# Routed experts in row blocks of 128, with one half of an expert's sums under the other

## The chip, the cores and the metric

One core of one Trainium2 chip runs the whole program; the other cores are idle. The metric is device time of one execution in microseconds (us). An execution of the kernel before took 560.33 us (median of 3 runs, 559.5 to 560.93).

## The reference

Three stages follow each other, on 1536 tokens (2 batches of 768) of 512 numbers:

```
attention   8 heads of 64; key j counts for query i if j < 4 or 0 <= i - j < 128; softmax; times v
dense       h = x @ w_in [512 x 2048];  g = max(0.01 h, h);  x = g @ w_out [2048 x 512]     (weights in float64)
routed      do = x @ w_skip > 0;  e = argmax(x @ w_gate) of 8 experts;  p = softmax(x @ w_gate)[e]
            out = x + p * (max(x @ w1[e], 0) @ w2[e])   for tokens with do, else out = x
            w1[e] 512 x 1024, w2[e] 1024 x 512
```

## The kernel before, in words

The program is first planned, then written out. Each piece of work is an operation with an engine, a modelled cost, a priority (`pr`, the lowest goes first), what it reads and writes, and buffers by tag; `Plan.run` walks a model of the five queues and emits operations in the order in which the model starts them. Each engine runs its own list in that order on the chip, whatever the real times are. So an operation that is late holds up everything behind it on its engine.

**Precision.** A product of two fp32 tensors is made from three fast products: each operand is split into a high part (a rounding copy, mostly on ACT) and a low part (the difference, on DVE or POOL): high x high, high x low, low x high. `split` (L693) does this for weights in SBUF, its copy at L701 and its difference at L708; `split_psum` (L1091) does it for tensors in PSUM, both at L1094 and L1095.

**Dense part.** Tokens go through in six groups of 256. For each group `chunk` (L822) runs 16 steps over the hidden columns: sums of `h` (L835), the activation, then sums into `acc` (L856). Attention of the next group is laid between the steps. After each group `gating` (L886) decides where its two tiles of 128 tokens go. It transposes x (L918), splits it (L921, L922), makes nine scores per token with `w9` (L930; one column for `w_skip`, eight for `w_gate`, 12 products a tile: three per 128 rows), copies them (L935), transposes them back (L937), and works out on DVE, in small steps (L947 to L992), the expert, the gate and the rank of each token among those of its expert, from counts that PE makes (L977). Tokens are then scattered by an indirect DMA of POOL into `scr`, 128 rows for each expert.

**The last group** (g = 5) is gated one tile at a time, on the way to the first expert. Expert 0's rows aren't read back from `scr`: `first_rows` (L801) loads those of the earlier groups, `first_x` (L810) adds the new ones on PE. Each of four column blocks `x0` gets a product of the rows loaded (L817), and one for each of the two new tiles, with a 0/1 matrix `sel` of that tile (L819). `sel` comes from DVE (L987) out of the ranks (L983). A plain fp32 product of PE stands in the trace as two instructions.

**Routed part** (`plan_routed`, L1019), eight experts one after the other: sums g1 of expert e, `hp` (L1066, two halves `a` of 512 columns, four blocks `k` of 128 rows, 24 products), the relu into `hs` (first half ACT L1070, second half DVE L1071), eight transposes (L1075, in two groups of four), the split into `gt`, the sums g2 into `yp` (L1082, 24 products), and the end: gate times `yp` plus x (L1085) and an indirect DMA to the output (L1087). Transposes of x for the next expert are L1059. Priorities put g1 of expert e + 1 ahead of g2 of expert e, and the transposes of `hs` between the second and third quarter of that g2.

**Weights of the experts** come in four tiles of 512 KB for each matrix (L1037), into raw buffers (`wm` four, `vs` one, `wf` one in two halves), and are split into pairs of `w` buffers. There are 32 `w` buffers, room for four matrices; the dense weights hold them until the last group's steps let them go. The order is W1 of expert 0, W1 of 1, W2 of 0, W1 of 2, W2 of 1, and so on; the low part of the last tile of a matrix is POOL's, the others are DVE's. A tile of w1 holds rows k, 4 + k, 8 + k, ... (partition p has row 4p + k), and of w2 partition p has rows 8p + 2n and 8p + 2n + 1. So all that meets them is cut with the same stride:

```
src = io["moe2_w2"][e].rearrange("(p j) d -> p j d", j=8) if m else io["moe2_w1"][e].rearrange("(p k) f -> p k f", k=4)
... tp.tile[:, k, :], xs.tile[:, k:512:4], c["idt"]          (x of an expert, L1059)
... tp.tile[:, j, :], hs.tile[:, 4 * b + j:1024:8], c["idt"]  (hs, L1075: both groups of four need both halves)
```

Of the kernel before, what the change touches and what calls it, by code (L numbers as in the profile page):

```python
# [225 lines left out]
class Arm:  # L226
# [63 lines left out]
    def keep(self):  # L290
# [7 lines left out]
        self.w9 = k("w9", [128, 2, 4, 9], F32R)  # L298
# [394 lines left out]
    def split(self, src, dst, at, n, pr, hi="ACT", lo="DVE", view=lambda t: t):  # L693
# [13 lines left out]
        P.op(hi, {"ACT": c_act(n, False), "DVE": c_dve2(n), "POOL": c_pool1(n)}[hi], f_hi, r=[src], w=[hk], pr=pr)  # L707
# [156 lines left out]
    def prepare(self, done):  # L864
# [9 lines left out]
        P.op("DVE", 90, lambda: nc.vector.tensor_copy(self.w9[:, 0], raw.tile), r=[raw], w=["w9"], pr=8)  # L874
        P.op("DVE", 100, lambda: nc.vector.tensor_tensor(out=self.w9[:, 1], in0=raw.tile, in1=self.w9[:, 0].bitcast(F32), op=ALU.subtract), r=[raw], w=["w9"], pr=8)
# [10 lines left out]
    def gating(self, g, acc, own):  # L886
# [9 lines left out]
        for i, t in zip(own, tiles):  # L896
            x = P.buf("x2", [128, 514])
            x2.append(x)
            for h in range(parts):
                q = slice(w * h, w * h + w)  # L900
                if (i if n > 1 else h) == 0:
                    P.op("ACT", c_act(w, True), lambda x=x, i=i, q=q: nc.scalar.activation(out=x.tile[:, q], in_=acc[i].tile[:, q], func=AF.Copy), r=[acc[i]], w=[(x, h)], pr=pr - 8)
                else:
                    P.op("DVE", c_dve(w), lambda x=x, i=i, q=q: V.tensor_copy(x.tile[:, q], acc[i].tile[:, q]), r=[acc[i]], w=[(x, h)], pr=pr - 8)
# [3 lines left out]
        lp = P.buf("T", [9, 128 * n])  # L908
        for m, x in enumerate(x2):
# [14 lines left out]
            for h in range(parts):  # L924
                ks = range(4 // parts * h, 4 // parts * (h + 1))

                def lg(m=m, xh=xh, ks=ks):
                    for k in ks:
                        for j, (a, b) in enumerate(((0, 0), (1, 0), (0, 1))):
                            nc.tensor.matmul(out=lp.tile[:, 128 * m:128 * m + 128], lhsT=self.w9[:, a, k, :], rhs=xh.tile[:, b, 128 * k:128 * k + 128],  # L930
                                             start=k == 0 and j == 0, stop=k == 3 and j == 2)

                P.op("PE", 3 * len(ks) * 54, lg, r=[(xh, (0, h)), (xh, (1, h)), "w9"], w=[lp], pr=pr)
        ls = P.buf("wl", [9, 128 * n])
# [13 lines left out]
        d(70, lambda: V.tensor_scalar(out=v(act, 1), in0=lt.tile[:, :, 0:1], scalar1=0.0, scalar2=None, op0=ALU.is_gt), [lt], [(s, "act")])  # L948
        for m in range(n):
            d(80, lambda m=m: V.scalar_tensor_tensor(out=cand()[:, m, :], in0=lt.tile[:, m, 1:9], scalar=one(mx, m), in1=c["em"][:, 0, :], op0=ALU.is_equal, op1=ALU.mult),  # L950
              [lt, (s, "mx")], [(s, ("cand", m))])
# [467 lines left out]
```

## Time and profile before

| | us |
|---|---|
| median of 3 runs (lowest, highest) | 560.33 (559.5, 560.93) |
| the profiled execution | 561.0 |
| its span, first to last instruction | 559.2 |
| PE busy in it | 521.8 (93%) |
| DVE, ACT, POOL busy | 415.9, 345.8, 166.9 |

The profile is one execution; its span is 1.8 us less than its time. Busy times of PE are those of matmuls (weight loads stand beside them as PEld). A line of a timeline merges like instructions that follow each other: its start, the time from there to the end of the last, and in brackets how long the engine had been idle and which instruction of another engine let it go on. The granted clock of PE is a share of full speed, 1.00 for 2.4 GHz and 0.50 for 1.2 GHz.

### The profile page before, as it was taken

How to read it: one execution, taken by the hardware profiler on the slowest of the kernel's cores; microseconds unless marked ns; L12 is line 12 of the kernel's file. 1: busy time of each engine (PE TensorE's matmuls, PEld its weight loads, DVE VectorE, ACT ScalarE, POOL GpSimd, SP SyncE). 2: the span in 40 equal slices, each digit the busy share in tenths (PEclk: the TensorE clock that was granted, in tenths of full speed). 3: DMA queues.
4: the chain of work that ended last, by engine and by line, in shares of the span. 5: the costliest groups of instructions: out<-in, count | busy, mean ns of one | idle time of the engine just before them, and what ended most of it. 6: DMA issues, size and time to landing. Idle time of an engine off the chain costs nothing.

```text
span 559.2 us, 10360 instructions
## 1 busy us (share of the span) xinstructions
PE 521.8 (93%) x3370; PEld 457.7 (82%) x3370; DVE 415.9 (74%) x1167; ACT 345.8 (62%) x899; POOL 166.9 (30%) x288
## 2 busy tenths in 40 slices
PE   3899999999998999989999999999999789999994
PEld 2778998888887888978888888988898668878883
DVE  3899999997667676777576876766856558998761
ACT  3998766655666656675556766465555367767650
POOL 4332022130264133333223333220221314354231
PEclk9999999999999999999999999999999899999998
DMA  7996344431111212232112320106565359879820
GB/s 179 308 349 234 130 154 139 136 104 38 50 39 30 68 30 45 50 83 49 29 24 51 85 49 16 24 1 221 164 213 184 128 193 319 301 236 353 277 79 19
DMA packets 80351, 72.46 MB, mean 130 GB/s; under 512 B 56563, under 2 KB 64755, under 8 KB 80288
## 3 DMA queue, kind: packets, MB, share of 16 engines
q1 hardware_dynamic: 78000, 70.54, 40.7%
q0 software_dynamic: 1600, 1.04, 0.6%
q8 instruction: 29, 0.48, 0.3%
q14 instruction: 34, 0.28, 0.2%
q10 hardware_dynamic: 688, 0.13, 0.1%
HBM read 65.40 MB, written 10.51 MB: 136 GB/s over the span
## 4 chain that ended last, share of the span: by engine, by line
PE 66%; DVE 14%; ACT 9%; issue 4%; DMA 3%; POOL 2%; POOLq 0%; SPq 0%; DVEq 0%; ACTq 0%
PE h L835 17%; PE acc L856 14%; PE acc L1082 7%; PE T L616 3%; PE PV L655 3%; PE h L1066 2%; DMA wm<-in_moe_w_dram 2%; PE S L1066 2%; PE PV L1066 2%; ACT P L588 2%; PE S L582 2%; DVE w L708 2%; PE T L930 1%; DVE C L671 1%; DVE P L585 1%
## 5 line engine op out<-in xcount | busy, mean ns | idle before, releaser
L835 PE MATMUL h<-x,w 128*128 128x256 f32 x1128 | 155.1, 286 | 0.1
L835 PEld LDWEIGHTS h<-x,w 128*128 128x128 f32 x1128 | 143.9, 190 | 4.3 <-DVE w L708 0.6
L856 PE MATMUL acc<-w,gh 128*128 128x512 f32 x308 | 100.2, 406 | 0.2 <-ACT gh L848 0.2
L588 ACT ACTIVATE P<-P,s 128x272 f32<-128x272 f32 (+1 forms) x96 | 50.2, 524 | 27.8 <-DVE s L585 26.4
L600 POOL TENSOR_SCALAR P<-P,s 128x272 f32<-128x272 f32 (+1 forms) x72 | 36.8, 523 | 93.8 <-DVE s L593 74.9
L856 PE MATMUL acc<-w,gl 128*128 128x512 f32 x156 | 61.5, 394 | 0.6 <-DVE gl L849 0.6
L856 PEld LDWEIGHTS acc<-w,gh 128*128 128x128 f32 x308 | 53.2, 189 | 7.9 <-ACT gh L848 0.6
L708 DVE TENSOR_TENSOR w<-wm,w 128x1024 fp32r<-128x1024 f32 x35 | 52.3, 1509 | 8.8 <-ACT w L701 8.0
L701 ACT ACTIVATE w<-wm 128x1024 fp32r<-128x1024 f32 x44 | 46.1, 1060 | 17.2 <-DMA wm<-in_moe_w_dram 6.8
L847 DVE TENSOR_TENSOR h<-h,t 128x256 f32<-128x256 f32 x94 | 40.2, 427 | 22.2 <-ACT t L846 21.7
L846 ACT ACTIVATE t<-h 128x256 f32<-128x256 f32 x94 | 35.7, 379 | 33.5 <-PE h L835 33.2
L848 ACT ACTIVATE gh<-h 128x256 fp32r<-128x256 f32 x92 | 34.9, 379 | 21.7 <-DVE h L847 20.9
L849 DVE TENSOR_TENSOR gl<-h,gh 128x256 fp32r<-128x256 f32 x92 | 38.6, 419 | 9.3 <-ACT gh L848 8.5
L701 ACT ACTIVATE w<-wf 128x512 fp32r<-128x512 f32 x52 | 31.8, 627 | 11.1 <-DVE wf L741 8.9
L585 DVE CUSTOM_DVE_ANT_0 P<-S,mk 128x272 f32<-128x272 f32 (+1 forms) x70 | 28.9, 413 | 11.3 <-PE S L582 7.9
L856 PEld LDWEIGHTS acc<-w,gl 128*128 128x128 f32 x156 | 29.3, 188 | 8.4 <-DVE gl L849 1.9
L708 POOL TENSOR_TENSOR w<-wm,w 128x1024 fp32r<-128x1024 f32 x9 | 22.3, 2477 | 44.5 <-PE h L835 15.2
L616 PE MATMUL T<-idt,P 128*128 128x128 f32 x152 | 27.2, 295 | 7.1 <-DVE kT L503 3.3
L616 PEld LDWEIGHTS T<-idt,P 128*128 128x128 f32 x152 | 22.3, 205 | 13.0 <-POOL P L600 4.3
L708 DVE TENSOR_TENSOR w<-wf,w 128x512 fp32r<-128x512 f32 x42 | 28.7, 694 | 0.7 <-ACT w L701 0.7
L671 DVE TENSOR_TENSOR C<-PV,C 64x256 f32<-64x256 f32 x48 | 20.3, 422 | 11.2 <-ACT C L670 8.1
L672 POOL TENSOR_TENSOR xr<-C 128x128 f32<-128x128 f32 x32 | 15.7, 490 | 43.0 <-DVE C L671 42.7
(267 smaller groups left out, 1117.0 us busy)
## 6 DMA issues: line engine op xcount, KB each, us to landing
wm<-in_moe_w_dram SPq DMA_DIRECT2D x44, 512.0 KB, 4.8
w<-in_moe_w_in_dram SPq DMA_DIRECT2D x14, 512.0 KB, 5.9
w<-in_moe_w_out_dram SPq DMA_DIRECT2D x14, 512.0 KB, 6.4
wf<-in_moe_w_dram SPq DMA_DIRECT2D x20, 256.0 KB, 5.0
vs<-in_moe_w_dram SPq DMA_DIRECT2D x10, 512.0 KB, 5.3
rq<-in_q_dram SPq DMA_DIRECT2D x56, 64.0 KB, 2.0
out_dram<-x SPq DMA_DIRECT2D x12, 256.0 KB, 2.9
rk<-in_k_dram SPq DMA_DIRECT2D x24, 96.0 KB, 2.1
```

The source lines that it names most:

```text
L588: P.op("ACT", 280 + 0.83 * ncol, lambda h=h: nc.scalar.activation(out=A.tile[:, 0:ncol, h], in_=A.tile[:, 0:ncol, h], func=AF.Exp, scale=- ...
L600: P.op("POOL", 245 + 0.83 * ncol, lambda h=h: nc.gpsimd.tensor_scalar(out=A.tile[:, 0:ncol, h], in0=A.tile[:, 0:ncol, h], scalar1=sm.tile[ ...
L616: nc.tensor.transpose(tt.tile[:, 2 * j + h, :], A.tile[:, o:o + 128, h], c["idt"])
L701: nc.scalar.activation(out=at(0), in_=view(src.tile), func=AF.Copy)
L708: P.op(lo, {"DVE": c_dve(n), "POOL": c_pool2(n)}[lo], lambda: eng[lo].tensor_tensor(out=at(1), in0=view(src.tile), in1=at(0).bitcast(F32), ...
L835: nc.tensor.matmul(out=h.tile, lhsT=wi.tile[:, a, 128 * k:128 * k + 128], rhs=xT.tile[:, b, k, :], start=k == 0 and n == 0, stop=k == self ...
L846: P.op("ACT", c_act(256, True), lambda: nc.scalar.activation(out=t.tile, in_=h.tile, func=AF.Copy, scale=0.01), r=[h], w=[t], pr=fast)
L847: P.op("DVE", c_dve(256), lambda: nc.vector.tensor_tensor(out=h.tile, in0=h.tile, in1=t.tile, op=ALU.max), r=[t], w=[h], pr=fast)
L848: P.op("ACT", c_act(256, True), lambda: nc.scalar.activation(out=gh.tile, in_=h.tile, func=AF.Copy), r=[h], w=[gh], pr=fast)
L849: P.op("DVE", c_dve(256), lambda: nc.vector.tensor_tensor(out=gl.tile, in0=h.tile, in1=gh.tile.bitcast(F32), op=ALU.subtract), r=[h, gh], ...
L856: nc.tensor.matmul(out=acc[i].tile, lhsT=a.tile[:, q], rhs=wo.tile[:, b, :], start=first and n == 0, stop=last and n == 2)
L1082: nc.tensor.matmul(out=yp.tile, lhsT=gt.tile[:, a, 2 * n + j, :], rhs=w2[n][b].tile[:, 512 * j:512 * j + 512], start=n == 0 and j == 0 and ...
```

## The change

1. Rows of the experts' weights are taken in blocks: tile k of w1 holds rows 128k to 128k + 127; a tile of w2 holds two such blocks, so that partition p has rows 256n + p and 256n + 128 + p, two pieces of 2 KB in place of one of 4 KB. The transposes of x and `hs` take contiguous columns, and each group of four transposes of `hs` reads one half of it.
2. g1 runs half by half: all 12 products of columns 0 to 511, then the 12 of 512 to 1023 (in two pieces of six; expert 0's first half in four of three). The relu and the transposes of a half wait for that half alone. For expert 0 the transposes and g2 get priorities just behind g1's first half, so g2 of expert 0 comes before g1 of expert 1, and W2 of expert 0 is loaded before W1 of expert 1.
3. `first_x` is made tile by tile: the four products of the loaded rows, then four of the first new tile, then four of the second.
4. Gating: `w9` holds high and low parts side by side, so one product with 18 columns does for two; 8 products a tile, the four with the high part of x apart from the four with the low part. The scores come back by a plain fp32 product with `fold`, which also adds the two parts. On DVE `sel` is made from the counts themselves ahead of the rank, and `act` after `cand`.
5. Two tiles of W1 of expert 2 (n = 2, 3) are split only after expert 0's columns, the last one's low part on DVE. A second copy of a tile half waits for the first. `fold` is one small POOL operation at the start.

```diff
@@ split @@
-    def split(self, src, dst, at, n, pr, hi="ACT", lo="DVE", view=lambda t: t):
+    def split(self, src, dst, at, n, pr, hi="ACT", lo="DVE", view=lambda t: t, after=()):
...
@@ first_x @@
-        for k, x in enumerate(self.x0):
-            P.op("PE", 220, lambda k=k, x=x: nc.tensor.matmul(out=x.tile, lhsT=xs0.tile[:, k:512:4], rhs=c["idt"], start=True, stop=False), r=[xs0], w=[x], pr=pr - 0.1)
-        for k, x in enumerate(self.x0):
-            P.op("PE", 440, lambda k=k, x=x: [nc.tensor.matmul(out=x.tile, lhsT=x2[i].tile[:, k:512:4], rhs=sel.tile[:, i, :], start=False, stop=i == 1) for i in range(2)],
-                 r=[(x2[i], h) for i in range(2) for h in range(2)] + [(sel, 0), (sel, 1)], w=[x], pr=pr)
+        for m, (x, cols) in enumerate([(xs0, lambda: c["idt"])] + [(x2[i], lambda i=i: sel.tile[:, i, :]) for i in range(2)]):
+            for k, x0 in enumerate(self.x0):
+                P.op("PE", 260, lambda k=k, x=x, x0=x0, m=m, cols=cols: nc.tensor.matmul(out=x0.tile, lhsT=x.tile[:, 128 * k:128 * k + 128], rhs=cols(), start=m == 0, stop=m == 2),
+                     r=[(x, h) for h in range(2)] + [(sel, m - 1)] if m else [xs0], w=[x0], pr=pr + (0.2, 0.1, 0)[m])
@@ gating @@
-            for h in range(parts):
-                ks = range(4 // parts * h, 4 // parts * (h + 1))
...
-                        for j, (a, b) in enumerate(((0, 0), (1, 0), (0, 1))):
...
-                P.op("PE", 3 * len(ks) * 54, lg, r=[(xh, (0, h)), (xh, (1, h)), "w9"], w=[lp], pr=pr)
+            for b in range(2):
+                for h in range(parts):
...
+                            nc.tensor.matmul(out=lp.tile[:, 128 * m:128 * m + 128], lhsT=self.w9[:, k, :, :].rearrange("p a e -> p (a e)"), rhs=xh.tile[:, b, 128 * k:128 * k + 128],
+                                             start=k == 0 and b == 0, stop=k == 3 and b == 1)
+                    P.op("PE", len(ks) * 66, lg, r=[(xh, (b, h)), "w9"], w=[lp], pr=pr)
...
-        P.op("PE", 30 * n, lambda: [nc.tensor.transpose(lt.tile[:, m, :], ls.tile[:, 128 * m:128 * m + 128], c["idt"][0:9, 0:9]) for m in range(n)], r=[ls], w=[lt], pr=pr)
+        P.op("PE", 200 * n, lambda: [nc.tensor.matmul(out=lt.tile[:, m, :], lhsT=ls.tile[:, 128 * m:128 * m + 128], rhs=c["fold"], start=True, stop=True) for m in range(n)], r=[ls], w=[lt], pr=pr)
...
+            if last:
+                i = own[0]
+                d(133, lambda cp=cp, i=i: V.tensor_scalar(out=self.sel.tile[:, i, :], in0=self.sel.tile[:, 2, :], scalar1=cp.tile[:, 0:1],
...
@@ plan_routed @@
-            src = io["moe2_w2"][e].rearrange("(p j) d -> p j d", j=8) if m else io["moe2_w1"][e].rearrange("(p k) f -> p k f", k=4)
+            src = io["moe2_w2"][e].rearrange("(j p) d -> p j d", j=8) if m else io["moe2_w1"][e].rearrange("(k p) f -> p k f", k=4)
...
+                    self.split(raw, ..., "ACT", "DVE" if n != 3 or e == self.E - 1 or (e, m) == (2, 0) else "POOL",
+                               after=[first] if (e, m) == (2, 0) and n > 1 else ())
...
-            if e + 1 < self.E:
-                weights(e + 1, 0, pr - 2.8)
-            weights(e, 1, pr - 1.5)
+            for ne, m in ((e, 1), (e + 1, 0)) if e == 0 else ((e + 1, 0), (e, 1)):
+                if ne < self.E:
+                    weights(ne, m, pr - (1.5 if m == (e > 0) else 2.8))
...
-            for k in range(4):
-                def g1(k=k, xt=xt, hp=hp, w1=w1):
-                    for a in range(2):
...
-                P.op("PE", 6 * c_mm(512), g1, r=..., w=hp + ([("g1", e)] if k == 2 else []), pr=pr + 0.01 * k)
+            for a in range(2):
+                for ks in ((0,), (1,), (2,), (3,)) if e == 0 and a == 0 else ((0, 1), (2, 3)):
...
+                    P.op("PE", 3 * len(ks) * c_mm(512), g1, r=...,
+                         w=[hp[a]] + ([("g1", e)] if a and ks[0] == 0 else []), pr=pr + 0.02 * a + 0.005 * ks[0])
...
-                P.op("PE", 4 * C_TR, ... hs.tile[:, 4 * b + j:1024:8] ..., r=[hs], w=[tp], pr=pr + 0.065)
+                P.op("PE", 4 * C_TR, ... hs.tile[:, 512 * b + 128 * j:512 * b + 128 * j + 128] ..., r=[(hs, b)], w=[tp], pr=pr + (0.065 if e else 0.01))
...
-                P.op("PE", 6 * c_mm(512), g2, ..., w=[yp], pr=pr + 3.55 + 0.01 * n)
+                P.op("PE", 6 * c_mm(512), g2, ..., w=[yp], pr=pr + (3.55 if e else 0.1) + 0.01 * n)
```

## Rows read from the trace of the kernel before

**Rows 1.** The page, part 4: the chain that ended last, shares by engine.

```profile
PE 66%; DVE 14%; ACT 9%; issue 4%; DMA 3%; POOL 2%; POOLq 0%; SPq 0%; DVEq 0%; ACTq 0%
```

**Rows 2.** Stretches of 10 us (columns as in the first line).

```profile
core 0: us, PE busy (x) PEld busy (x) DVE busy (x) ACT busy (x) POOL busy (x), PEclk, DMA share, GB/s
450.00:460.00 10.00, 8.24 (x40) 6.28 (x39) 6.12 (x10) 6.97 (x10) 2.37 (x1) 1.00 0.69 229
...
490.00:500.00 10.00, 8.79 (x43) 7.14 (x42) 10.00 (x12) 6.62 (x9) 4.44 (x3) 1.00 0.69 208
```

**Rows 3.** Timeline of PE, last gating to the first expert's transposes.

```profile
434.24 0.73 PE L817 MATMUL acc<-idt,xs 128*128 128x128 f32 x2 [0.24 <-DVE x L904]
434.81 0.60 PE L918 MATMUL T<-idt,x 128*128 128x128 f32 x4
...
440.13 0.88 PE L930 MATMUL T<-wl,w 128*9 128x128 f32 x12 [1.40 <-DVE sm L959]
...
442.88 0.17 PE L977 MATMUL PV<-oh_all,tri 128*128 128x8 bf16 x1 [1.22 <-DVE oh_all L954]
...
455.38 1.13 PE L1075 MATMUL T<-idt,hs 128*128 128x128 f32 x8 [1.52 <-ACT hs L1070]
```

**Rows 4.** The chain in order of time (start, us; merged).

```profile
392.17 1.44 PE T L930 x24
...
443.37 2.10 PE h L819 x8
445.47 1.87 PE acc L819 x8
447.35 1.28 PE S L1066 x3
448.62 1.09 PE PV L1066 x3
...
543.05 8.38 PE acc L1082 x36
```

**Rows 5.** Stretches of 1 us, columns as in rows 2.

```profile
442.00:443.00 1.00, 0.12 (x5) 0.11 (x5) 0.96 (x11) 0.30 (x2) 0.68 (x1) 0.77 0.03 8
...
449.00:450.00 1.00, 1.00 (x5) 0.79 (x4) 0.00 (x0) 0.48 (x1) 0.00 (x0) 0.82 0.00 0
```

**Rows 6.** Timeline of DVE: the second tile's rank and its selection.

```profile
443.09 0.17 DVE L983 CUSTOM_DVE_ANT_0 sm<-PV,oh_all 128x8 f32<-128x8 f32 x1
...
443.30 0.34 DVE L987 TENSOR_SCALAR hs<-hs,rank_all 128x128 f32<-128x128 f32 x1
```

**Rows 7.** Timelines of ACT and DVE: relu and split of the first expert.

```profile
454.68 0.58 ACT L1070 ACTIVATE hs<-S 128x512 f32<-128x512 f32 x1
...
456.73 1.29 DVE L1095 TENSOR_TENSOR x<-T,x 128x512 fp32r<-128x512 f32 x2 [1.50 <-ACT x L1094]
```

**Rows 8.** Timeline of all engines, 485 to 493 us: relu of expert 3.

```profile
485.81 1.21 DVE L708 TENSOR_TENSOR w<-vs,w 128x1024 fp32r<-128x1024 f32 x1
...
487.50 4.06 DVE L708 TENSOR_TENSOR w<-wm,w 128x1024 fp32r<-128x1024 f32 x1 [0.47 <-ACT w L701]
...
487.92 2.54 POOL L708 TENSOR_TENSOR w<-wf,w 128x512 fp32r<-128x512 f32 x2
...
492.08 0.68 DVE L1071 TENSOR_SCALAR hs<-h 128x512 f32<-128x512 f32 x1
...
492.90 1.13 PE L1075 MATMUL T<-idt,hs 128*128 128x128 f32 x8 [1.21 <-DVE hs L1071]
```

**Rows 9.** Timelines of DVE and PE: W1 of expert 5, low parts and use.

```profile
492.68 3.51 DVE L708 TENSOR_TENSOR w<-wm,w 128x1024 fp32r<-128x1024 f32 x2
...
509.04 4.25 PE L1066 MATMUL h<-w,wl 128*128 128x512 f32 x18
```

**Rows 10.** The page, part 6: DMA issues (KB each, us to landing).

```profile
wm<-in_moe_w_dram SPq DMA_DIRECT2D x44, 512.0 KB, 4.8
w<-in_moe_w_in_dram SPq DMA_DIRECT2D x14, 512.0 KB, 5.9
```

More of the change, by code (lines that the diff above doesn't have):

```diff
@@ L705, in f_hi @@
                 nc.gpsimd.tensor_scalar(out=at(0), in0=view(src.tile), scalar1=1.0, scalar2=1.0, op0=ALU.mult, op1=ALU.mult)
-        P.op(hi, {"ACT": c_act(n, False), "DVE": c_dve2(n), "POOL": c_pool1(n)}[hi], f_hi, r=[src], w=[hk], pr=pr)
+        P.op(hi, {"ACT": c_act(n, False), "DVE": c_dve2(n), "POOL": c_pool1(n)}[hi], f_hi, r=[src], w=[hk], pr=pr, after=after)
         P.op(lo, {"DVE": c_dve(n), "POOL": c_pool2(n)}[lo], lambda: eng[lo].tensor_tensor(
@@ L947, in gating @@
         d(85, lambda: V.tensor_reduce(out=v(mx, 1), in_=lgt(), op=ALU.max, axis=AX.X), [lt], [(s, "mx")])
-        d(70, lambda: V.tensor_scalar(out=v(act, 1), in0=lt.tile[:, :, 0:1], scalar1=0.0, scalar2=None, op0=ALU.is_gt), [lt], [(s, "act")])
         for m in range(n):
@@ L951, in gating @@
               [lt, (s, "mx")], [(s, ("cand", m))])
+        d(70, lambda: V.tensor_scalar(out=v(act, 1), in0=lt.tile[:, :, 0:1], scalar1=0.0, scalar2=None, op0=ALU.is_gt), [lt], [(s, "act")])
         d(85, lambda: V.tensor_reduce(out=v(mi, 1), in_=cand(), op=ALU.min, axis=AX.X), [(s, ("cand", m)) for m in range(n)], [(s, "mi")])
@@ L982, in gating @@
             rk = self.rank_all[:, tiles[m]:tiles[m] + 1]
+            if last:
+                i = own[0]
+                d(133, lambda cp=cp, i=i: V.tensor_scalar(out=self.sel.tile[:, i, :], in0=self.sel.tile[:, 2, :], scalar1=cp.tile[:, 0:1],
+                                                          scalar2=self.sel.tile[:, 3, i:i + 1], op0=ALU.is_equal, op1=ALU.mult),
+                  [cp, (self.sel, 2), (self.sel, ("own", i))], [(self.sel, i)])
             d(80, lambda m=m, rk=rk, cp=cp: V.tensor_tensor_reduce(out=cand()[:, m, :], in0=cp.tile, in1=oh(m), op0=ALU.mult, op1=ALU.add,
                                                                    scale=1.0, scalar=0.0, accum_out=rk), [cp, ("oh", tiles[m])], [(s, ("cand", m)), ("rank", tiles[m])])
-            if last:
-                i = own[0]
-                d(133, lambda rk=rk, i=i: V.tensor_scalar(out=self.sel.tile[:, i, :], in0=self.sel.tile[:, 2, :], scalar1=rk,
-                                                          scalar2=self.sel.tile[:, 3, i:i + 1], op0=ALU.is_equal, op1=ALU.mult),
-                  [("rank", tiles[m]), (self.sel, 2), (self.sel, ("own", i))], [(self.sel, i)])
             d(70, lambda m=m, rk=rk: V.tensor_scalar(out=one(far, m), in0=rk, scalar1=128.0, scalar2=OOB, op0=ALU.is_ge, op1=ALU.mult),
@@ L1036, in weights @@
                     raw = P.buf(tag, [128, 1024 // k])
-                    P.op("SP", C_DMA, lambda raw=raw, sv=sv, q=q: nc.sync.dma_start(out=raw.tile, in_=sv[:, q]), w=[raw], pr=pr - 16, lat=512 * 1024 / 310.0 / k)
-                    self.split(raw, [(x, i) for x in hl], lambda j, hl=hl, q=q: hl[j].tile[:, q], 1024 // k, pr + 0.3 * n, "ACT", "DVE" if n != 3 or e == self.E - 1 else "POOL")
+                    P.op("SP", C_DMA, lambda raw=raw, sv=sv, i=i, k=k: nc.sync.dma_start(
+                        out=raw.tile.rearrange("p (j d) -> p j d", d=512), in_=sv[:, i:i + 1, :] if k == 2 else sv), w=[raw], pr=pr - 16, lat=512 * 1024 / 310.0 / k)
+                    self.split(raw, [(x, i) for x in hl], lambda j, hl=hl, q=q: hl[j].tile[:, q], 1024 // k, pr + 0.3 * n, "ACT", "DVE" if n != 3 or e == self.E - 1 or (e, m) == (2, 0) else "POOL",
+                               after=[first] if (e, m) == (2, 0) and n > 1 else ())
                 W[e, m].append(hl)
@@ L1074, in plan_routed @@
                 tp = P.buf("T", [128, 4, 128])
-                P.op("PE", 4 * C_TR, lambda hs=hs, tp=tp, b=b: [nc.tensor.transpose(tp.tile[:, j, :], hs.tile[:, 4 * b + j:1024:8], c["idt"]) for j in range(4)], r=[hs], w=[tp], pr=pr + 0.065)
+                P.op("PE", 4 * C_TR, lambda hs=hs, tp=tp, b=b: [nc.tensor.transpose(tp.tile[:, j, :], hs.tile[:, 512 * b + 128 * j:512 * b + 128 * j + 128], c["idt"]) for j in range(4)], r=[(hs, b)], w=[tp], pr=pr + (0.065 if e else 0.01))
                 self.split_psum(tp, (gt, b), lambda i, gt=gt, b=b: gt.tile[:, i, 4 * b:4 * b + 4, :], 512, pr - 3)
@@ L1336, in constants @@
     G.affine_select(out=idt, in_=one, compare_op=ALU.is_equal, fill=0.0, base=0, pattern=[[-1, 128]], channel_multiplier=1)
+    fold = T("fold", [18, 9])
+    G.tensor_tensor(out=fold, in0=idt[0:18, 0:9], in1=idt[0:18, 9:18], op=ALU.add)
     G.iota(dif, pattern=[[-1, 128]], base=0, channel_multiplier=1, allow_small_or_imprecise_dtypes=True)
```

38 lines of the change are left out of this document (20 added, 18 removed).

## The prediction

> **What bounds the kernel now.** I read the shares of the chain first: PE holds 66% of it, DVE 14% [rows 1]. Then the windows of 10 us over the end of the program, where nearly all of the change lies: PE isn't full in the first expert's stretch and in one other, and DVE has 3.88 us to spare in the first and nothing in the second [rows 2]. The timeline of PE gives the holes: 1.40 and 1.22 us while the last tile is gated, 1.52 us before the first expert's transposes [rows 3], and 1.21 us before those of expert 3, where the relu on DVE came late [rows 8]. The chain in order of time shows sixteen instructions of `first_x` (eight fp32 products) as 3.97 us right before the first expert's sums [rows 4]. Last, windows of 1 us with the clock: the mean of 0.77 in 442 to 443 and of 0.82 in 449 to 450 put the fall to half speed (1.2 GHz) at 442.54 and the rise at 449.36 [rows 5]; ahead of the fall PE had the two holes of the gating, after it no hole. So: from 434 to 447 a chain of small steps over PE, ACT and DVE, afterwards PE with few holes.
>
> **The change part by part.** Sums are made against the profiled execution's own 561.0 us (its span of 559.2 and 1.8 around it), which is 0.67 above the median of 560.33; the forecast is for the median.
>
> *Gating of the first five groups.* 24 products take 1.44 us, 60 ns each [rows 4]. Eight fewer save 0.48 a group. The two folds take the place of two transposes; a fold is a plain fp32 product of two instructions. The trace has none with nine columns; with 128 columns two take 0.47 at half speed (1.87 for eight [rows 4]), so at most 0.23 at full speed, and I take 0.11 more than the transpose it replaces, its middle. That is 0.48 - 0.22 = 0.26 a group, some 1.2 for five, as PE is in the chain there. Ends: 2.4 gained with free folds; a loss of 1.1 (0.22 by five) if products with 18 columns of weights take 90 ns in place of 60, by which nothing is saved. Taken -1.2, since the nearest row is the product itself.
>
> *Gating of the last two tiles.* Of the second tile's 12 products, all issued after 440.13 [rows 3], only two need the last low part; ten by 60 ns is 0.6 off the chain. The fold adds 0.1. `sel` no longer waits for the rank: 443.09 to 443.30, 0.2 off [rows 6]; zero if the read of the counts in PSUM eats it. The products of the loaded rows get a priority behind the first tile's transposes; before, 0.57 passed from the one to the other [rows 3], between 0 and 0.57 may go, I take 0.3. Sum -1.0, ends 0 and -1.6. The move of `act` and the second copy that waits are under 0.1 and hidden: one follows what it needs anyway, the other already followed the first copy.
>
> *First columns.* The four products of the first new tile go into the hole of 1.22 us [rows 3]; they need 0.9 at full speed (half of 1.87 [rows 4]). Behind the second selection four products stay, not eight: -1.9 at the clock of the trace. If they were put ahead of the second tile's scores on PE, up to 0.9 comes back. The split of the first column (one ACT and one DVE step) lies beside the other three products as long as those run at half speed.
>
> *The clock takes half of this back.* The first expert's sums start at 447.35 [rows 4]; 1.0 + 1.9 earlier is 444.45, still inside 442.54 to 449.36 [rows 5]. What PE does earlier in there it does at half speed, so 2.9 us are worth 1.45 at its end. Taken -1.45; both ends are a rival below.
>
> *Half an expert's sums under the other half.* For expert 0 the hole of 1.52 us [rows 3] goes: relu (0.58) and split of a half (0.65 on DVE [rows 7]) and four transposes lie beside 12 products of 0.23 [rows 4], 2.8 us, and then two quarters of g2 cover the second half. Taken -1.5; some 0.5 would stay if the split ends last. For the later experts g2 of the expert before covers already; the first four transposes of a group no longer wait for DVE's relu and stand as 0.4 us more cover before the second four. That takes 0.4 off the 1.21 at expert 3 [rows 8]. Ends -1.2 and the give-back below.
>
> *Weights.* Pieces of 2 KB for w2: 512 KB in pieces of 1 KB land in 5.9 us, in pieces of 4 KB in 4.8 [rows 10], so between 0 and 1.1 us more a tile. It is hidden: the last low part of W1 of expert 5 that DVE makes ends at 496.19 and is used at 509.04, 12.85 us later [rows 9]. The same margin covers that a half-by-half g1 lets go of its first `w` buffers after three quarters of its products, not one (2.8 us later), and the other load order, as all four first matrices lie in SBUF before the last gating. Without that cover each of the later tiles would cost up to 1.1. Two low parts of 1.21 [rows 8] come to DVE behind the first columns, into the spare 3.88 us [rows 2]: 0. Contiguous columns for the transposes: the strided ones do eight in 1.13 with the tail, contiguous ones four in 0.60 [rows 3]; 0. The constant at the start lies under the first loads: 0.
>
> On one point row and skill are weighed. A low part of 1.21 us took 4.06 when POOL made two of its own (2.54 us) beside it [rows 8], and the relu stood behind it. The Trainium skill, in SBUF — State Buffer, section Who interferes with whom, says that a DVE instruction with two SBUF inputs and a GpSimd instruction that reads SBUF don't share the port but block one another; the trace agrees, 1.21 + 2.54 being most of 4.06. By that rule the low part that the change takes from POOL can't hold DVE up any more, and by it the sum would be some 2.5 us of DVE time better and not a PE time; what speaks against the change is that PE running ahead presses the remaining ones closer together, which is the fourth case below, priced there from rows.
>
> Sum: -1.2 - 1.45 - 1.5 - 0.4 = -4.55; 561.0 - 4.55 = 556.45, less 0.67: 555.8.
>
> **Rivals.**
> 1. The clock stays up: PE's holes of 1.40 and 1.22 [rows 3] get the first tile's products and fewer waits. Then the 2.9 us count in full, the first six sums take 1.4 and not 2.37 (-1.0), the four last columns 0.9 less, and the split of the first column shows with 0.5: -1.2 - 2.9 - 1.0 - 0.4 - 1.5 - 0.4 = -7.4, 552.9. Against it: the chain of the second tile still runs over DVE, and PE must wait for it.
> 2. Given back at expert 3: DVE is full in 490 to 500 [rows 2], and if its line up to the relu at 492.08 [rows 8] doesn't come earlier, PE waits there for all that it gained after 434. Only the first groups' 1.2 stays: 559.1. Against it: DVE's line starts from buffers that PE lets go, and has 3.88 us spare at 450 to 460 [rows 2].
> 3. The change doesn't do its main step: the order puts the first four transposes behind all of g1, or W2 of expert 0 is late. Then the 1.5 stays: 557.3.
> 4. Slower: DVE becomes the bound of experts 1 to 4. Its line gets two more low parts (2.4) and starts 2.8 later, since buffers are let go later; if this isn't met by spare time, the relu of expert 3 is late by 5.2 more: -1.2 + 5.2, 561.0 + 4.0 - 0.67 = 564.3. It decides from the point where DVE has less than 5.2 us idle between the first columns and expert 2's relu. For it: 10.00 of 10 in 490 to 500. Against it: the margin of 12.85 us [rows 9] and the spare 3.88.
>
> **How the numbers follow.** Forecast 0.45, clock up 0.20, given back 0.17, main step missing 0.08, slower 0.10. What a measurement of this kernel can tell from no change is about 0.3%, 1.7 us: faster means under 558.65, slower over 562.0. Faster: 0.43 + 0.20 + 0.05 + 0.07 = 0.75; the same: 0.02 + 0.12 + 0.01 = 0.15; slower 0.10. The range leaves out the slower case and an edge of the others: it goes from 550.5 (clock up, with free folds and no hole left) to 560.8 (given back, with dear folds). The likeliest case alone: 553.5 to 558, from the ends of its own terms.
>
> **What would show it.** PE reaches the first g1 near 444.5 less the 1.2 of the groups; a stretch at 0.50 is there again and ends near 449; no hole over 0.5 between g1 and g2 of expert 0; eight instructions of `first_x` behind the second selection, not sixteen; g2 of expert 0 ahead of g1 of expert 1. L930 products stay at 60 ns, and folds under 0.25 each. The experts' part, first sum to last, takes 0.5 less than before (1.9 of holes, less 1.45 spent more at half speed). It is wrong if transposes of experts 1 to 5 wait for DVE's relu by more than 3 us together, if low parts of weights end within 3 us of their use, or if the first five groups take longer.

## The result and the profile after

| | before | after |
|---|---|---|
| median, us (lowest, highest, runs) | 559.99 (559.5, 560.93, 4) | 551.21 (550.55, 553.42, 4) |
| the profiled execution, us | 561.0 | 550.55 |
| its span, us | 559.2 | 548.8 |

The ratio is 0.985, 95% interval [0.982, 0.987]: 8.8 us less. The forecast was 555.8, so 4.5 less than the median that it was made against (560.33). The direction was right and the time lies in the range, but the gain is about twice the forecast.

The first view is the two traces cut at the same places: the first and the last sum of `h` in the dense part (L835 before, L834 after), the first g1 product, the end of the last product. The last sums into `acc` fall into the second stretch. Before:

```profile
core 0: us, PE busy (x) PEld busy (x) DVE busy (x) ACT busy (x) POOL busy (x), PEclk, DMA share, GB/s
24.80:426.43 401.63, 388.29 (x2691) 348.17 (x2690) 306.91 (x959) 256.52 (x738) 113.14 (x225) 1.00 0.32 97
426.43:447.00 20.57, 17.18 (x127) 14.57 (x125) 12.99 (x58) 8.77 (x23) 4.12 (x3) 0.89 0.44 145
447.00:551.41 104.41, 101.26 (x478) 83.15 (x477) 81.01 (x90) 65.33 (x88) 38.46 (x22) 0.99 0.69 236
```

After:

```profile
25.23:423.13 397.90, 386.66 (x2662) 347.67 (x2660) 306.04 (x959) 256.76 (x738) 112.18 (x225) 1.00 0.33 99
423.13:440.50 17.37, 15.33 (x120) 12.57 (x119) 11.21 (x53) 6.51 (x21) 1.00 (x1) 0.92 0.33 110
440.50:540.58 100.08, 99.29 (x478) 81.33 (x477) 79.08 (x96) 66.27 (x91) 40.20 (x22) 1.00 0.76 256
```

Length less PE's busy time is PE's idle time. The dense part gives 3.7 us (2.1 of them idle time), the last gating with the first columns 3.2, the experts 4.3 (2.4 of them idle). What lies before and behind takes 0.9 back: 10.4 in all between these two executions. That is 1.6 more than between the medians, since this execution of before is 1.0 above its median and this one of after 0.7 below.

In the page's part 4 PE's share of the chain is up from 66% [rows 1], so less of the chain is other engines:

```profile
PE 74%; DVE 11%; ACT 7%; issue 3%; POOL 2%; DMA 2%; POOLq 0%; SPq 0%; DVEq 0%; ACTq 0%
```

PE's timeline after, from the last tile's scores to the first g2, answers to [rows 3] and [rows 4]:

```profile
435.56 0.64 PE L930 MATMUL T<-wl,w 128*18 128x128 f32 x8 [1.45 <-DVE sm L949]
...
436.93 0.71 PE L818 MATMUL h<-hs,x 128*128 128x128 f32 x4
437.48 0.77 PE L818 MATMUL acc<-hs,x 128*128 128x128 f32 x4
...
438.78 1.22 PE L818 MATMUL h<-hs,x 128*128 128x128 f32 x4 [0.16 <-DVE hs L985]
439.79 1.06 PE L818 MATMUL acc<-hs,x 128*128 128x128 f32 x4
440.50 3.35 PE L1070 MATMUL S<-w,wl 128*128 128x512 f32 x12
443.69 1.53 PE L1070 MATMUL PV<-w,wl 128*128 128x512 f32 x6
445.05 0.60 PE L1080 MATMUL T<-idt,hs 128*128 128x128 f32 x4
445.41 1.64 PE L1070 MATMUL PV<-w,wl 128*128 128x512 f32 x6
447.83 0.66 PE L1080 MATMUL T<-idt,hs 128*128 128x128 f32 x4 [0.79 <-DVE hs L1076]
```

The hole of 1.40 is still there (1.45), that of 1.22 is filled with the first tile's columns, that of 1.52 has become 0.79. Behind the second selection there are eight instructions, not sixteen: 1.72 us to the first g1, where it was 3.77 (443.23 to 447.00).

The clock, in stretches of 1 us as in [rows 5]:

```profile
437.00:438.00 1.00, 1.00 (x9) 0.98 (x9) 0.93 (x9) 0.28 (x2) 0.00 (x0) 0.90 0.00 0
438.00:439.00 1.00, 0.84 (x16) 0.62 (x14) 1.00 (x11) 0.02 (x1) 0.97 (x1) 0.50 0.07 16
...
441.00:442.00 1.00, 1.00 (x5) 0.79 (x4) 0.48 (x4) 1.00 (x2) 0.00 (x0) 0.89 0.00 0
```

By the means of 0.90 and 0.89 half speed (1.2 GHz) lasts from 437.80 to 441.2. That is 3.4 us, half of the 6.8 of before, and it ends 0.7 into the first g1, not 2.4.

### The profile page after: what moved, and what is told of

Same layout as the page of the kernel before. It is cut to its first block, busy times and chain, and to the rows that moved or that the text cites. A ratio compares the mean times of both kernels' runs of the same rounds, so it can differ in the third digit from the quotient of the medians.

```text
span 548.8 us, 10276 instructions
## 1 busy us (share of the span) xinstructions
PE 516.7 (94%) x3334; PEld 453.5 (83%) x3334; DVE 411.6 (75%) x1168; ACT 344.8 (63%) x899; POOL 164.7 (30%) x288
## 4 chain that ended last, share of the span: by engine, by line
PE 74%; DVE 11%; ACT 7%; issue 3%; POOL 2%; DMA 2%; POOLq 0%; SPq 0%; DVEq 0%; ACTq 0%
PE h L834 19%; PE acc L855 15%; PE acc L1087 8%; PE h L1070 4%; PE PV L655 4%; PE T L616 3%; PE S L1070 2%; PE PV L1070 2%; PE S L582 2%; DVE C L671 2%; ACT P L588 2%; PE S L855 1%; DVE kT L503 1%; PE PV L855 1%; PE T L1080 1%
## 5 line engine op out<-in xcount | busy, mean ns | idle before, releaser
L834 PE MATMUL h<-x,w 128*128 128x256 f32 x1128 | 154.6, 286 | 0.3 <-DVE x L708 0.2
L834 PEld LDWEIGHTS h<-x,w 128*128 128x128 f32 x1128 | 144.0, 190 | 4.9 <-DVE w L708 0.6
L708 DVE TENSOR_TENSOR w<-wm,w 128x1024 fp32r<-128x1024 f32 x36 | 49.0, 1367 | 4.1 <-ACT w L701 3.5
L708 POOL TENSOR_TENSOR w<-wm,w 128x1024 fp32r<-128x1024 f32 x8 | 19.7, 2460 | 43.0 <-ACT w L701 22.2
L616 PE MATMUL T<-idt,P 128*128 128x128 f32 x152 | 26.9, 293 | 3.7 <-DVE kT L503 2.9
L616 PEld LDWEIGHTS T<-idt,P 128*128 128x128 f32 x152 | 22.3, 205 | 8.3 <-issue 4.1
L622 ACT ACTIVATE AT<-T 128x256 fp32r<-128x256 f32 x60 | 20.1, 381 | 12.0 <-PE T L616 11.3
```

The lines of the kernel that those rows point to most:

```text
L616: nc.tensor.transpose(tt.tile[:, 2 * j + h, :], A.tile[:, o:o + 128, h], c["idt"])
L708: P.op(lo, {"DVE": c_dve(n), "POOL": c_pool2(n)}[lo], lambda: eng[lo].tensor_tensor(out=at(1), in0=view(src.tile), in1=at(0).bitcast(F32), ...
L834: nc.tensor.matmul(out=h.tile, lhsT=wi.tile[:, a, 128 * k:128 * k + 128], rhs=xT.tile[:, b, k, :], start=k == 0 and n == 0, stop=k == self ...
```

## The experiments

Each was timed beside the kernel before. "Dense", "gating" and "experts" are the three stretches above, and "idle" is PE's idle time in one, all from each one's profile. The changed kernel has four executions, from 550.55 to 553.42, timed apart from these. So a difference of 1 or 2 us between an experiment and it isn't sure, and where the ratios to the kernel before give another size than the medians, both are named.

**1. The score form alone** (`scores_only`): the kernel before with the change's hunks on `w9`, `lp`, `lg` and `fold`, in all gatings.

```
- for h in range(parts): ... 12 products of 9 columns, reading both parts
+ for b in range(2): for h in range(parts): ... 4 products of 18 columns, reading part b
- 2 transposes
+ 2 products with fold
```

> The kernel before with the new form of the scores in all gatings alone (18 columns of weights, high and low part apart, fold). Between the two profiles the six dense groups end 3.7 us earlier, and PE's idle time in them is 2.1 us less. Theory order: the new pieces on PE give another order of the dense part, whose waits are fewer, so this alone gives all of it: dense part 3.7 us shorter, and with 0.6 from the last gating some 4 us in all, 556. Theory work: only products count, eight fewer a group at 60 ns less the folds, 1.6 us in the five groups; the rest of the dense gain then belongs to the weights' order or to chance, and the kernel takes 557.5 to 558. Forecast on record: 1.2 for the groups and 0.5 for the end, 558.3.

Measured: 556.89, ratio 0.994 [0.992, 0.996]. Its three stretches:

```profile
27.00:424.92 397.92, 386.68 (x2662) 347.63 (x2660) 305.97 (x959) 256.71 (x738) 112.18 (x225) 1.00 0.33 97
424.92:445.71 20.79, 17.69 (x120) 14.98 (x119) 13.10 (x58) 8.76 (x23) 3.35 (x2) 0.84 0.44 144
445.71:549.13 103.42, 100.22 (x478) 82.21 (x477) 80.54 (x90) 65.28 (x88) 38.36 (x22) 1.00 0.71 238
```

Dense and its idle time (11.24) are as after, the gating as before. The experts' 1.0 less goes with the clock, which was back at full speed here when they began. So the score form is enough for the whole dense gain.

**2. The routed part alone** (`routed_only`): `plan_routed` and `split` of the changed kernel, `first_x` in its old order but with contiguous columns.

> The kernel before with the routed part of the change alone (row blocks, half by half, expert 0's priorities and load order, two late splits; the first columns as before but over contiguous columns). Theory holes: the waits of 1.5 and 0.2 at expert 0 and some of the 1.4 later go, contiguous transposes give under 0.5: 2.0 to 3.0 us, 557 to 558, with the half-speed stretch as long as before (6.8 us). Theory clock: the experts' part of the changed kernel is 4.3 us shorter mostly because the half-speed stretch is half as long (3.4 for 6.8), which comes from the gating and not from here: then this kernel gains 1.5 to 2.0 and shows the stretch of 6.8.

Measured: 554.78, 0.991 [0.989, 0.992]: 5.0 us, more than either case expected. Experts 99.66, idle 0.78. The half-speed stretch was 3.4 us here, not the 6.8 that was expected. Experiment 8 takes this part to pieces.

**3. First columns tile by tile alone** (`columns_only`): strided columns, selection still from the rank.

```
+ for m, (x, cols) in enumerate([(xs0, ...)] + [(x2[i], ...) for i in range(2)]):
+     for k, x0 in enumerate(self.x0): ... x.tile[:, k:512:4] ... pr=pr + (0.2, 0.1, 0)[m]
```

> The kernel before with the first columns made tile by tile alone (strided columns, selection still from the rank). The forecast on record: four products leave the path, 1.9 us at half speed, of which the half-speed stretch takes back half: 1 us, 559. Theory clock: with the first tile's products in the hole of 1.2 us the stretch gets shorter or goes, then 2 to 3.5 us, 556.5 to 558. Theory nothing: the first columns wait for the second tile's chain anyway, and the products move beside it without shortening it: within 0.5.

Measured: 559.74, 0.999 [0.998, 1.000]. The first tile's products went into the hole, but the clock fell at 440.72, so that they ran at half speed and on past its end, and held up the second tile's counts by 0.9 us; the gating came to 19.89:

```profile
440.43 0.22 PE L936 MATMUL T<-idt,wl 9*128 9x9 f32 x1
440.77 1.31 PE L818 MATMUL h<-hs,x 128*128 128x128 f32 x4
441.87 1.14 PE L818 MATMUL acc<-hs,x 128*128 128x128 f32 x4
442.81 0.21 PE L976 MATMUL PV<-oh_all,tri 128*128 128x8 bf16 x1
```

By itself this step is worth nothing that can be measured.

**4. PE work put back into the scores** (`scores_padded`): the changed kernel with two repeated transposes in each tile of the first five groups, an estimated 2.2 us of PE time.

```
- for k in ks:
+ for k in ([0, 1] if n > 1 else []) + list(ks):
```

> The changed kernel with two transposes more in each tile of the first five gatings (made twice, the same result), about 0.22 us a tile, which is what four of the saved products take; the order stays. Theory work: the 2.2 us of added PE work come back in full, 553.4. Theory order: the dense gain is of waits, not of work; the added work falls into PE's remaining holes and costs under 1.2, 552 to 552.4.

Measured: 553.46, 0.988 [0.987, 0.990]: 2.3 above the changed kernel. In its profile PE is busy 1.9 longer in the dense part, and that part is 1.8 longer (399.66); its idle time there is 11.11, as after. So with this order work on PE costs about its own length, and putting it in doesn't undo the gain in idle time.

**5. Order without fewer products** (`parts_only`): the kernel before, with its twelve products a tile in two steps.

```
+ for b in range(2):
+     for k in ks:
+         for a in ((0, 1), (0,))[b]: ... lhsT=w9[:, a, k], rhs=xh[:, b, k]
+     r=[(xh, (b, h)), "w9"]
```

> The kernel before with its twelve products a tile in two steps: eight of the high part, which no longer wait for the low part, and then four of the low. Count, columns and transposes are unchanged. If what the new scores gain in the dense part comes from not waiting for the low part and the order that follows, about 1.2 us of idle time goes (dense 400.4 to 400.7 where it was 401.6 or 400.75): 558.5 to 559 where the kernel before has 560. If it comes from the sixteen products saved a group and the shorter rows behind them, this does nothing (560, ratio 1.000), and the dense part's idle time stays at 12.7 to 13.3.

Measured: 556.07, 0.993 [0.991, 0.996]: 3.9 us, more than either case expected (a group saves eight products, not the sixteen that the expectation names). Its dense part:

```profile
24.77:422.24 397.47, 386.86 (x2691) 348.67 (x2690) 304.81 (x959) 256.34 (x738) 112.20 (x225) 1.00 0.33 98
```

That is all of the gain of experiment 1 with not one product less. What PE waited for in the dense part (us, times, longest), before:

```profile
PE T L616 <- DVE kT L503: 3.3, 7, 0.7
PE T L616 <- POOL xr L672: 1.8, 1, 1.8
PE T L616 <- POOL P L600: 1.5, 2, 0.9
```

And with the twelve products in two steps:

```profile
PE T L616 <- DVE kT L503: 3.0, 7, 0.6
PE T L931 <- DVE wl L922: 1.3, 1, 1.3
...
PE T L616 <- POOL P L600: 0.6, 1, 0.6
```

Before, PE never stood still ahead of a score product (no L930 among its waits); now it does, for 1.3. What went is idle time ahead of the attention's transposes of P (L616), 7.1 us in all before and 3.7 now. The two waits of 1.8 and 0.9 for POOL stand in the traces of the kernel before and of experiments 2, 3 and 8, and in none of experiments 1, 5, 6 and the changed kernel. In the planner's model the steps of the scores became ready at other times, and the attention's work fell into another order on PE.

**6. The same in the changed kernel** (`after_parts`): its scores replaced by those of experiment 5, no fold.

> The changed kernel with twelve products of nine columns a tile and the transposes of before, but with the eight products of the high part ahead, not waiting for the low part, and the four of the low part behind. If the dense part's gain comes from that order alone, as the kernel before with only this edit says (dense 397.47), this is as fast as the changed kernel: dense part 397.5 to 398, 551.2 (550.5 to 552), ratio 0.985. If fewer products matter where nothing else hides them, it gives back the net 0.8 us by which the first five groups' products and folds differ in duration, and is near 552. Rival: the folds on the last tiles' chain were a loss of 0.3 to 0.4 us, and it is faster than the changed kernel, near 550.8 (0.983).

Measured: 551.67, 0.986 [0.983, 0.988]; dense 397.79, idle 10.21. A group's folds in the timeline of the changed kernel:

```profile
393.24 0.61 PE L937 MATMUL T<-fold,wl 18*128 18x9 f32 x4
393.78 1.46 PE L834 MATMUL h<-x,w 128*128 128x256 f32 x10
```

And the two transposes that stood there before:

```profile
395.01 0.28 PE L937 MATMUL T<-idt,wl 9*128 9x9 f32 x2
395.23 0.73 PE L856 MATMUL acc<-w,gh 128*128 128x512 f32 x2
```

From the first's start to the next instruction's that is 0.54 against 0.22. Eight fewer products save 0.48 a group (60 ns each [rows 4]; 62 after), so the net is 0.16 a group, 0.8 us for five. PE is indeed busy 0.9 longer in this dense part than in the changed kernel's (387.57 for 386.66), but idle 1.0 less, so these runs can't tell the net from nothing. Nor do they decide the rival: the gating is 16.59 here and 17.37 in the changed kernel, but this execution has no stretch at half speed in it.

**7. The changed kernel with the old scores** (`scores_undone`).

> The changed kernel with the scores of all gatings as before (twelve products of nine columns a tile, a transpose and no fold). If the parts add, it gives back what the scores gave by themselves, 3.1 us: about 554.3, ratio 0.990, with the dense part (first dense product to last) back near 400.7 to 401.6 us and PE's idle time there at 12.7 or more. If the score form is worth only the 1.2 us of the forecast, it lands near 552.4 (0.987). Rival: the score form hid behind the other parts and costs nothing here (551.2).

Measured: 554.23, 0.989 [0.986, 0.993]: 3.0 above the changed kernel by the medians, 2.7 by the ratios; dense 400.78, idle 12.70. The dense part is back where the old scores have it.

**8. Row blocks alone** (`blocks_only`): the kernel before with the change's weight layout and contiguous columns, order and waits as before.

```
- w2[e].rearrange("(p j) d -> p j d", j=8)   - xs.tile[:, k:512:4]
+ w2[e].rearrange("(j p) d -> p j d", j=8)   + xs.tile[:, 128 * k:128 * k + 128]
```

> The kernel before with the weights' rows in blocks of 128 and so with contiguous columns in all transposes of the routed part and the first columns; order, priorities and waits as before. By the forecast this is worth 0 (559.9, ratio 1.000). If contiguous columns are what shortens the 56 transposes of a full program and the step from them to the next product, as the changed kernel's profile shows (hidden size about 1.0 us), it gives 558.9 (0.998), and the experts' part falls from 104.4 to about 103.4 with its idle time still 3.1. Rival: smaller pieces of a load (2 KB) make the later weights late: PE then waits on a weight's high or low part in experts 2 to 5, and it is over 561.

Measured: 556.44, 0.994 [0.991, 0.996]: 3.5 us, where the forecast had 0 and the expectation 1.0 at most. Its three stretches:

```profile
24.79:425.36 400.57, 387.87 (x2692) 348.27 (x2690) 306.81 (x959) 256.08 (x738) 112.70 (x225) 1.00 0.33 98
425.36:444.89 19.53, 16.21 (x126) 13.51 (x125) 12.90 (x58) 8.76 (x23) 4.03 (x3) 0.86 0.48 156
444.89:546.72 101.83, 100.04 (x478) 81.70 (x477) 80.54 (x90) 64.93 (x88) 37.57 (x22) 0.99 0.71 242
```

The order on PE is that of before, yet it works 1.0 us less in the gating and 1.2 less in the experts, and waits 1.4 less there. (The dense part's 1.1 less is mostly an excess of the one execution of before, see below.) First, the columns. These are the loaded row's products, the one that [rows 3] shows at 434.24 with 0.73 for two:

```profile
432.92 0.49 PE L817 MATMUL acc<-idt,xs 128*128 128x128 f32 x2 [0.22 <-DVE x L904]
```

From their start to the next instruction the four took 0.26, 0.25, 0.57 and 0.48 before, 0.15, 0.14, 0.33 and 0.25 here; with 0.29 off the sixteen last instructions that is the 1.0. In the experts a transpose of `hs` or `xs` comes 110 ns behind the one ahead of it (116 before), and the product behind the last transpose 28 ns later (36), which comes to 0.5. Some 0.45 more of the 1.2 is the clock: the half-speed stretch reached 1.5 us into the experts' sums here, 2.4 before. The rest of the 1.2 was not located. On the columns the Trainium skill, in Advanced Engine Details and Errata, section SBUF Cachelines, says that accesses which each fall on another 16-byte line are slower; columns four and eight fp32 apart are 16 and 32 bytes apart, and the trace agrees.

Second, the hole of 1.21 at expert 3 [rows 8] is gone. ACT's waits ahead of the high parts of `wm`, in the experts' part (last column: idle before, and for what), before:

```profile
L701 ACT ACTIVATE w<-wm 128x1024 fp32r<-128x1024 f32 x32 | 33.4, 1060 | 8.4 <-DMA wm<-in_moe_w_dram 5.3 <-PE acc L1082 1.6 <-PE PV L1066 0.6
```

Row blocks alone, the same group, and `wm` in the page's part 6:

```profile
L701 ACT ACTIVATE w<-wm 128x1024 fp32r<-128x1024 f32 x32 | 33.2, 1059 | 6.5 <-DMA wm<-in_moe_w_dram 3.5 <-PE acc L1083 1.6 <-PE PV L1067 0.6
...
wm<-in_moe_w_dram SPq DMA_DIRECT2D x44, 512.0 KB, 4.5
```

The loads land sooner (4.8 before [rows 10]; the traces have the landing of 22 of the 44 before and of 36 here), and ACT's high parts follow sooner. On DVE the low part that took 4.06 ahead of expert 3's relu had started 0.42 ahead of POOL's [rows 8]. Here it starts 0.97 ahead and takes 1.22. The long ones now stand behind that relu (POOL's line is beside DVE's):

```profile
484.02 1.22 DVE L708 TENSOR_TENSOR w<-wm,w 128x1024 fp32r<-128x1024 f32 x1
...
484.99 2.66 POOL L708 TENSOR_TENSOR w<-wf,w 128x512 fp32r<-128x512 f32 x2
...
486.00 0.69 DVE L1072 TENSOR_SCALAR hs<-h 128x512 f32<-128x512 f32 x1
486.61 5.48 DVE L708 TENSOR_TENSOR w<-wm,w 128x1024 fp32r<-128x1024 f32 x2
```

The Trainium skill, in Perfetto Trace Analysis, section DMA Optimizations, holds that going from 2 KB to 4 KB a transfer can do much for throughput. The traces don't show it here: after 440 us a packet of 2 KB took 97 ns in the mean in this run and one of 4 KB 193 ns before, the same for each byte. Nor is it the smaller pieces that land sooner. `wm` tiles of W1, whose pieces stay 4 KB, took 4.75 us in the mean (7 known landings after 440 us), and 5.76 in experiment 5 (7), which has the old rows and the same order of loads; those of W2, in pieces of 2 KB, took 4.74 here and 5.33 there (15 each). What the edit changes for W1 is that a tile is one stretch of 512 KB in memory, where its rows lay 16 KB apart. Why the loads land sooner was not isolated.

**9. The halves undone** (`halves_undone`): the changed kernel with g1 in its old block order and transposes waiting for both halves.

```
+ for k in range(4): for a in range(2): ... three products
- r=[(hs, b)]
+ r=[hs]
```

> The changed kernel with g1 in the old order (block by block, both halves together) and transposes that wait for both halves; row blocks and all else stay. Theory holes: the waits before expert 0's transposes and its g2 are there again, 1.5 to 2.0 us, as its g2 has nothing ahead of it to cover them: 553 to 553.5. Rival: other experts' work fills them, and half by half is worth under 0.5: 551.2 to 551.7.

Measured: 552.82, 0.985 [0.983, 0.988]: 1.6 above the changed kernel by the medians, but with the same ratio to the kernel before, so the time alone doesn't show what the halves are worth. The trace shows the wait at expert 0 again, now behind the transposes, at the split; PE's idle time in the experts is 1.68 (0.79 in the changed kernel):

```profile
PE acc L1085 <- DVE x L1098: 1.5, 1, 1.5
```

**10. Expert 0 undone** (`e0_undone`): the changed kernel with the priorities and load order of before for expert 0.

```
- weights(ne, m, pr - (1.5 if m == (e > 0) else 2.8)) ... pr + (0.065 if e else 0.01) ... pr + (3.55 if e else 0.1)
+ weights(ne, m, pr - (1.5 if m else 2.8))            ... pr + 0.065                  ... pr + 3.55
```

> The changed kernel with expert 0's priorities and load order as before: W1 of expert 1 ahead of W2 of expert 0, transposes and g2 of expert 0 behind the first sums of expert 1. Theory holes: half by half alone covers little for expert 0 if something else has to run meanwhile; the first sums of expert 1 do that as well, so within 0.7 of the changed kernel: 551 to 552. Rival: W2 and the priorities are what takes the holes away; then 1.5 us come back: 552.7.

Measured: 553.98, 0.988 [0.985, 0.991], above the changed kernel by 2.8 (medians) or 1.9 (ratios). PE's waits for the relu are 2.2 in all where the changed kernel has 0.79: half by half needs these priorities or the load order, which were undone together. Another 0.75 of the profile is the clock, whose half-speed stretch reached 2.2 us into the first sums here.

```profile
PE T L1080 <- DVE hs L1076: 2.2, 2, 1.8
```

**11 and 12. The holes of the gating filled** (`after_filled`, `before_filled`): closed fp32 products on a tile that is overwritten later, five in the changed kernel's hole of 1.45, five and four in the two holes of the kernel before (not five each, as the expectation says).

```
+ for after in [self.mark] * 5:
+     P.op("PE", 260, ... matmul(out=self.x0[0].tile, ..., start=True, stop=True), pr=pr + 0.05, after=[after])
```

> The changed kernel with PE kept at work in the hole of 1.45 us ahead of the second tile's scores: five products of the loaded rows made again (nothing else changes). Theory clock: the hole is what lets the clock fall; with it filled there is no stretch at 0.50 before the end, and the 3.4 to 6.8 us at half speed give back 1.0 to 2.5 us: 548.7 to 550. Rival: the clock falls all the same, since PE is short of work in all of the gating; then the filler costs nothing or up to 0.5: 551 to 551.7.

Measured: 550.39, 0.982 [0.979, 0.984]. No window of the gating or the experts is at half speed, and the mean granted clock was 0.995 to 0.997 in all six executions, where the changed kernel has 0.990 to 0.995. The first g1 starts at 439.48, 1.0 earlier. Then 1.2 is lost at expert 1, whose tokens are not back yet:

```profile
PE acc L1064 <- DMA xs<-scr: 1.2, 1, 1.2
```

It is the fastest kernel of the study by its median, but its interval overlaps the changed kernel's. Nor is the hole alone what lets the clock fall: experiment 6 keeps a hole of 1.4 there, and its profiled execution has no half-speed stretch behind it; two of its six executions are at 0.996, four at 0.990 or 0.991.

> The kernel before with its two holes of 1.40 and 1.22 us filled in the same way (five products each). Theory clock: no stretch at 0.50, so the eight products of the first columns and the first sums run at full speed: 3.0 us less, 556.8. Rival: the stretch stays; within 0.5 of before.

Measured: 562.18, 1.003 [1.000, 1.005], slower than either case expected. Eight instructions of fillers took 2.1 us in front of the second tile's counts, which came 18.1 us behind the last sum of `h` (16.5 before); the clock stayed up in the gating and fell for 3.4 us at 458.3, behind the first expert's hole. Filling costs more than the clock gives where the fillers delay the chain.

## Why the prediction fell short

Forecast and measured, in us; the last two columns are from the profiles above and from the runs.

| term of the sum | forecast | profiles | shown by |
|---|---|---|---|
| first five groups | -1.2 | -3.7 | 1, 5, 6, 7: mostly order, not products; some 0.9 of it is the one execution of before |
| last gating chain | -1.0 | -1.15 | -0.7 of it are contiguous columns (8) |
| first columns | -1.9 | -2.05 | -0.15 to -0.3 of it are contiguous columns (8); alone the step is worth nothing (3) |
| clock gives back half | +1.45 | -0.8 | stretch 3.4, not 6.8; not surely the change's |
| holes of experts 0 and 3 | -1.9 | -2.4 | 8 (expert 3), the traces of 9 and 10 (expert 0) |
| contiguous columns in the experts | 0 | -1.15 | 8 shows -0.8 without the clock's share, -0.5 of it in the transposes' steps |
| start and tail | 0 | +0.9 | not followed; the first sum of `h` starts at 24.8 to 25.2 us in eleven of the profiles and at 26.4 to 27.0 in three |

*First five groups.* The step that failed is the mechanism: "Eight fewer save 0.48 a group", less the folds. Its bookkeeping was nearly right (net 0.8, not 1.2), but by experiment 5 the gain comes with no product less, and experiment 6 can't tell the net from nothing. What pays is the order that follows from the high part's products not waiting for the low part. Four other kernels with the old scores (2, 3, 7 and 8) have dense parts of 400.6 to 400.8, so 401.63 holds 0.9 of that one execution (a hole of 0.55 at 390.98 is in it alone); the order is worth 2.7 to 3.3 by the profiles, 2.9 to 3.9 by the medians of 1 and 5. Whether another small change of these priorities would do as well was not tried.

*Weights and contiguous columns.* The second failed step, costed at 0 twice: row blocks alone gave 3.5 us (8). The zero for contiguous columns came from comparing eight strided transposes with four contiguous ones, with their tails [rows 3]; the row that answered stood in the same group, a strided product of two instructions with 0.73. And "between 0 and 1.1 us more a tile" for pieces of 2 KB bounded the loads by the wrong sign: its rows of 1 KB and 4 KB pieces belong to other tensors at other times, and it took no account of W1's rows, which now lie side by side. A gain should have been inside the bound. Row blocks are the largest single part of the routed change, 3.5 of its 5.0.

*Last gating.* The sum of the two terms was nearly right (-3.2 against -2.9), in part by luck: 0.85 to 1.0 of it are contiguous columns, which the forecast had at 0, and one cause was wrong. Ten of twelve products were to leave the chain; all eight still stand behind the hole, at 435.56. The releaser is DVE's L949, which reads the first tile's scores in one of the two `T` buffers, and the second tile's scores need that buffer. On DVE's timeline after, the second tile's last low part ends only 0.14 before L949:

```profile
435.00 0.41 DVE L921 TENSOR_TENSOR wl<-T,wl 128x256 fp32r<-128x256 f32 x1
435.33 0.22 DVE L949 SCALAR_TENSOR_TENSOR sm<-T,sm,em 128x8 f32<-128x8 f32 x1
```

That the buffer is the cause is read from the releaser and the code, and was not run. The first columns went as forecast: eight instructions, not sixteen.

*The clock.* "2.9 us are worth 1.45" supposed that the stretch stays where it is and as long. After, it came 4.7 us earlier and was half as long, so rival 1 is half true: the clock didn't stay up, but took nothing back. How long it is differs from one execution to the next (below), and in experiments 4, 9 and 10, whose last gating is the changed kernel's, it is 6.8 us again. So the 0.8 us are not sure to be the change's.

*Half by half.* Expert 0 was to lose its hole of 1.5 and kept 0.79, by DVE's relu; the bound named 0.5, by the split. At expert 3 the forecast took 0.4 off 1.21 by earlier transposes. All of it went, and it goes with row blocks alone (8); in experiment 9 it stays away without the halves. That earlier landings did it is read from the waits in experiment 8, not isolated.

*The rivals on the slow side.* DVE did not become the bound: its low parts of `wm` from 450 to 545 us take 1.42 us in the mean after (1.61 before), and PE waits for nothing there (before, 1.4 us for DVE's relu in these 95 us). Rival 2 fails by the same rows.

*The signs.* Three came: the eight instructions of `first_x`, g2 of expert 0 ahead of g1 of expert 1, and score products near 60 ns. The others missed: the first g1 starts at 440.50, not near 443.3; the half-speed stretch ends at 441.2, not near 449; 0.79 stays where no hole over 0.5 was to be; a fold takes 0.27, not under 0.25; and the experts' part is 4.3 shorter, not 0.5. Whether low parts end 3 us ahead of their use was not followed.

The parts add within the noise. By medians the score form is 2.9 (1) or 3.0 (7), its order alone 3.9 (5), row blocks 3.5, the rest of the routed part 1.5 (2 less 8), the columns 0.1: 8.0 to 9.0 for the 8.8 measured.

## What to carry to other kernels

An edit costed at nothing needs a bound on both sides from a row of the same form of operation: here the two zeros, a layout and its loads, were worth as much as the parts that the sum was about. Where a planner orders the work, time the edit once with its order and without its arithmetic, as experiment 5 does, before the saving is put down to fewer instructions. Read where an old hole's wait really ends (a buffer, a load) before counting what moves out from behind it.

## What the runs showed of the hardware

- The half-speed stretch that begins in or behind the gating was 6.83, 3.41 or 0 us long in the fourteen profiles, and the mean granted clock differs between executions of one kernel: 0.986 to 0.994 for the kernel before; in experiment 6 two executions with 0.996 took 549.15 and 549.65, four with 0.990 or 0.991 took 551.28 to 553.51. Two kernels that are 1 or 2 us apart can't be told apart by one execution of each.
- An fp32 product whose 128 weights lie 16 bytes apart takes 0.26 to 0.57 us to the next instruction, 0.14 to 0.33 where they are contiguous, at full speed.
- Weight tiles of 512 KB (`wm`) issued after 440 us land in 5.5 to 6.1 us (medians of the kernel before and of experiments 3, 5 and 12) with the old rows, and in 4.5 to 5.3 with row blocks (2 and 6 to 11). The changed kernel's own median of 3.7 over all such loads rests on 6 known landings of 44.
